# A fused attention and feed-forward kernel: lower parts, sums and stores listed elsewhere around the second product

## The chip, the cores and the metric

The kernel runs as one program on one core of a Trainium2 chip. The metric is the device time of one execution in microseconds. Before the change it is 1362.32 us, the median of 3 runs (1361.0 to 1362.66).

A core has five engines that matter here. TensorE (PE in the profile; its weight loads are PEld) multiplies matrices into PSUM. VectorE (DVE), ScalarE (ACT) and GpSimd (POOL) work on elements. SyncE (SP) only issues transfers (DMA). Each engine works through its own list of instructions in order, and waits at an instruction until what that instruction needs is done.

## The reference

```python
scores = scale * np.matmul(q, k.transpose(0, 1, 3, 2))
thresh = np.max(scores, axis=-1, keepdims=True) - tau
scores = np.where(scores >= thresh, scores, -1000000000.0)
attn = softmax(scores)                      # written out in the reference
x = (attn @ v)  ->  [4608 tokens, 512]
h = x @ w_in                                # 512 -> 2048
g = h * np.tanh(log1p(exp(h)))              # Mish
out = g @ w_out                             # 2048 -> 512
```

There are 8 batches of 8 heads, 576 positions and 64 elements a head. The first part up to x is the attention; `x @ w_in` is called the first product here, `g @ w_out` the second. Both weights arrive as 64-bit floating point numbers.

## The kernel before, in words

**Number formats.** A matrix product is made of three products of numbers split in two: each operand has an upper part in a short format and a lower part, the rest (operand minus upper part). The products upper x upper, upper x lower and lower x upper are summed in PSUM. ScalarE makes the upper parts (a cast), VectorE the lower parts (a subtraction); so a split is one ScalarE and one VectorE instruction, and the second needs the first.

**Decoding w_out.** The second weight is taken in 8 pieces, j = 0 to 7, of 128 x 1024 elements. `load_w` (line 187) brings the 64-bit words, `convert` (197) has ScalarE turn both halves into numbers, `compose` (202) has VectorE do three bit operations and GpSimd one addition, `upper_w` (212) casts on ScalarE, `lower_w` (215) subtracts on VectorE. In the profile the bit operations write `s`, `a`, `s`, the addition is `s<-s,w` on POOL, the parts are `w2h` and `w2l`.

**Units.** The attention ends near 917 us. What is left then is the first product of the last batch, 384 matmuls of 288 columns. The code deals it out in 32 units u of 12 matmuls (loop at line 804; the first four blocks of h have their last quarter held back, so the first three units finish none and unit 3 finishes four blocks, and then each unit finishes one). Between the units the table `steps` names other work: the decoding of w_out by `COMPOSE` = (0, 3, 7, 10, 14, 17, 21, 24), loads of h back from memory (`load_z`), Mish (`combine`), the split of g (`split_z`). Within a unit, the work of the table comes first, in the order in which it was put into the table, and then the 12 matmuls with what leaves them.

**How h leaves.** Each of the 32 blocks of h goes to one of 8 PSUM banks and from there into a buffer `hst`, copied by VectorE (even blocks) or ScalarE (odd blocks). A bank can be used again when it has been copied out. A buffer takes four blocks, and there are two buffers. After each fourth block `store` (545) writes the buffer to memory in two transfers.

**The second product.** It runs over 9 groups of 512 tokens (c), each over 8 pieces of the weight (j); n = 8 c + j counts the 72 steps of the loop at line 853. For c = 0 a step has 24 matmuls of 512 columns. For c > 0 the product is arranged as seven smaller products of 42 matmuls of 256 columns a step, which need four combinations of the weight's quarters: `sums_w` (219) makes them with four VectorE instructions into the free half of a z buffer, `split_w` (227) splits them (`sh` on ScalarE, `sl` on VectorE). Both run once, during c = 0. The z buffers, five of them, take turns; `load_z(n)` needs the buffer that step n - 5 had, which is free when the sums of that step are split (c = 0) or its g is split (c > 0). In each step ScalarE does Mish for step n + 3, then the upper g of step n + 2, then the upper sums of a step; after the last step of c = 0 VectorE and ScalarE copy four banks out.

**What sets the order.** The class `InOrder` (82) makes TensorE, VectorE, ScalarE and GpSimd keep the order in which the code issues. SyncE isn't wrapped, so the order of its transfers is that of the scheduler that builds the program. Because all instructions of the four engines pass through one helper, the profile shows line 92 for them; the groups are told apart by the names of their tiles.

Of the kernel before, what the change touches and what calls it, by code (L numbers as in the profile page):

```python
# [15 lines left out]
B, H, S, D = 8, 8, 576, 64  # L16
# [19 lines left out]
HB = S // 2  # L36
NBLK = 2 * B
NJ = NF // 2
# [3 lines left out]
COMPOSE = (0, 3, 7, 10, 14, 17, 21, 24)  # L42
# [35 lines left out]
def fv(ap):  # L78
    return ap.bitcast(F32)
# [78 lines left out]
def attention_moe(tc, q, k, v, tau, w_in, w_out, out):  # L158
    nc = tc.nc
    from contextlib import ExitStack  # L160

    with ExitStack() as outer:
# [56 lines left out]
        def sums_w(j):  # L219
            y = z[j]  # L220
            a11, a21, a12, a22 = (whole[j][:, i * QT:(i + 1) * QT] for i in range(4))
            nc.vector.tensor_tensor(y[:, 4], a21, a22, ALU.add)
            nc.vector.tensor_tensor(y[:, 6], a21, a11, ALU.subtract)
            nc.vector.tensor_tensor(y[:, 5], y[:, 4], a11, ALU.subtract)
            nc.vector.tensor_tensor(y[:, 7], a12, y[:, 5], ALU.subtract)

        def split_w(j):
            y = z.pop(j)[:, 4:].rearrange("p n t -> p (n t)")
            ws[j] = [
                homes["wl"].tile([P, 4 * QT], F32R, name=f"sh{j}"),  # L230
                homes["wr"].tile([P, 4 * QT], F32R, name=f"sl{j}", tag=f"sl{j}"),
            ]
            nc.scalar.copy(ws[j][0], y)
            nc.vector.tensor_tensor(ws[j][1], y, fv(ws[j][0]), ALU.subtract)

        def load_z(n):
            if n < NG:
                c, j = divmod(n, NJ)
                z[n] = scratch(CYCLE[n % 5], "z").rearrange("p (n t) -> p n t", t=QT)
                if c == 0:  # L240
                    for i in range(2):
                        nc.sync.dma_start(z[n][:, i:4:2], hd[i][:, j])
                else:
                    for at, i in ((0, 2 * c + 1), (2, 2 * c)):
                        nc.sync.dma_start(z[n][:, at:at + 2], hd[i][:, j])
# [21 lines left out]
        nc = Engines(tc)  # L267
        with ExitStack() as first:
# [6 lines left out]
            with ExitStack() as att:  # L275
# [269 lines left out]
                def store(queue, hst, at, f):  # L545

                    half, j = divmod(f, NJ)
                    off, end = 0, HB
                    while off < end:
                        i, to = divmod(at + off, QT)  # L550
                        m = min(QT - to, end - off)
                        queue.dma_start(hd[i][:, j:j + 4, half, to:to + m], hst[:, :, off:off + m])
                        off += m

                def gemm1(b, xs, bank=shared, first=1):

                    halves = (range(NF // 2), range(NF // 2, NF))  # L560
                    if b < B - 1:
                        order = [(c, f) for c in range(2) for fs in halves for f in fs]
                    else:
                        order = [(c, f) for fs in halves for c in range(2) for f in fs]
                    banks = {}
                    made = {}

                    def parts(c, f, ds):
                        if (c, f) not in banks:
                            banks[c, f] = bank("h")  # L570
                        h = banks[c, f]
                        half, at = divmod(f * P, DF // 2)
                        for d in ds:
                            xh, xl = xs[d][c]
                            wh, wl = (w[:, d, at:at + P] for w in w1[half])
                            for i, (a, m) in enumerate(((wh, xh), (wh, xl), (wl, xh))):
                                nc.tensor.matmul(
                                    h[:, :HB], a, m, start=d == 0 and i == 0, stop=d == ND - 1 and i == 2
                                )
                                yield  # L580

                    def leave(c, f):
                        if f % 4 == 0:
                            made["hst"] = hp.tile([P, 4, HB], F32, name="hst", tag="hst")
                        hst, h = made["hst"], banks.pop((c, f))
                        if b < B - 1 or f % 2:
                            nc.scalar.copy(hst[:, f % 4], h[:, :HB])
                        else:
                            nc.vector.tensor_copy(hst[:, f % 4], h[:, :HB])
                        if f % 4 == 3:  # L590
                            store(nc.sync if b < B - 1 else nc.scalar, hst, (2 * b + c) * HB, f - 3)

                    for c, f in order[:first]:
                        yield from parts(c, f, range(ND - 1))
                    for n, (c, f) in enumerate(order):
                        steps = parts(c, f, range(ND - 1, ND) if n < first else range(ND))
                        for i in range(3 if n < first else 3 * ND):
                            next(steps)
                            if i == (2 if n < first else 3 * ND - 1):
                                leave(c, f)  # L600
                            yield
# [183 lines left out]
            def at(u, *work):  # L785
                steps.setdefault(u, []).append(work)

            for j, u in enumerate(COMPOSE):
                if j >= 3:
                    at(COMPOSE[j - 3] + 2, load_w, j)  # L790
                    at(u - 2, convert, j)
                at(u, compose, j)
                at(u + 3, upper_w, j)
                at(COMPOSE[j + 1] if j + 1 < NJ else u + 4, lower_w, j)
            for n, u in enumerate((19, 20, 22, 25, 28)):
                at(u, load_z, n)
            for n, u in enumerate((22, 26, 29)):
                at(u, combine, n)
            at(24, split_z, 0)
            for _ in stream:  # L800
                pass
            stream = gemm1(B - 1, batches[B - 1], bank, 4)
# [50 lines left out]
        for n in range(NG):  # L853
            c, j = divmod(n, NJ)
            combine(n + 3)
            for i in range(n + 1 + (n > 0), n + 3):
                split_z(i)
            if n < NJ:
                sums_w(n)
                split_w(n)  # L860
            load_z(n + 5)
            if j == 0:
                banks = [bank("o") for _ in range(4 if c == 0 else len(PRODUCTS))]
            if c == 0:
                gh, gl = (x.rearrange("p n t -> p (n t)") for x in gs.pop(n))
                wh, wlo = wa[j]
                order = [(e, d) for e in range(2) for d in range(ND)]
                if j == NJ - 1:
                    order.sort(key=lambda at: at[1])
                for e, d in order:  # L870
                    cols = slice(2 * e * QT + d * P, 2 * e * QT + (d + 1) * P)
                    toks = slice(2 * e * QT, 2 * (e + 1) * QT)
                    for i, (x, y) in enumerate(((wh, gh), (wh, gl), (wlo, gh))):
                        nc.tensor.matmul(
                            banks[d], x[:, cols], y[:, toks],
                            start=j == e == i == 0, stop=j == NJ - 1 and e == 1 and i == 2,
                        )
                    if j == NJ - 1 and e == 1:
                        if d % 2 == 0:
                            pair = [x.rearrange("p n t -> p (n t)") for x in held()]  # L880
                        value = pair[d % 2]
                        if d % 2:
                            nc.vector.tensor_copy(value, banks[d])
                        else:
                            nc.scalar.copy(value, banks[d])
                        nc.sync.dma_start(out[d * P:(d + 1) * P, :2 * QT], value)
                continue
            for k, (wi, gi) in enumerate(PRODUCTS):
                o = banks[k].rearrange("p (n t) -> p n t", t=QT)
                w, at = (wa[j], (0, 2, 3)[wi]) if wi < 3 else (ws[j], wi - 3)  # L890
                for b in range(2):
                    cols = slice(at * QT + b * P, at * QT + (b + 1) * P)
                    for i, (x, y) in enumerate(((0, 0), (0, 1), (1, 0))):
                        nc.tensor.matmul(
                            o[:, b], w[x][:, cols], gs[n][y][:, gi],
                            start=j == b == i == 0, stop=j == NJ - 1 and b == 1 and i == 2,
                        )
                if j == NJ - 1:
                    leave(k, c, o)
            gs.pop(n)  # L900
# [46 lines left out]
```

## Time and profile before

| what | us |
|---|---|
| median of 3 runs | 1362.32 |
| profiled execution: its time | 1362.23 |
| profiled execution: its span | 1360.4 |
| PE busy | 1322.8 |
| DVE busy | 1112.4 |
| ACT busy | 989.4 |
| POOL busy | 874.3 |

The profile is one execution. Its span reaches from the first to the last instruction; the device time has about 1.8 us around it. Times in the views are counted from the start of the span. A row of the timeline gives start, length, engine, line, operation, tiles written and read, and in brackets how long the engine was idle before it and what ended that. The chain of waits is followed back from the last instruction: at each step it names what released it. The granted clock (PEclk) is TensorE's clock as a share of its full speed.

The stretch in question is from 917 us, when the attention has ended, to about 1043 us. From there on TensorE works without a gap until 1351.8 us.

### The profile page before, as it was taken

The page shows a single profiled execution, that of the slowest core. Times are in us where ns is not written, and L with a number is a line of the kernel's source. Part 1 is how long each engine was busy: PE and PEld are TensorE (multiplying, and loading weights), DVE is VectorE, ACT ScalarE, POOL GpSimd, SP SyncE. Part 2 cuts the span into 40 slices and gives each one's busy share as a digit, 9 for nine tenths or more (in the row PEclk, how much of TensorE's full clock was granted, in tenths as well). Part 3 has the DMA queues.
Part 4 walks back from the last instruction along what each step waited for, and adds up shares of the span by engine and source line. Part 5 has one row for each costly group of instructions (what it writes and reads, how often), then busy time and mean ns, then how long its engine had stood idle before and what let it go on. Part 6 is the DMA issues. An engine that isn't in the chain of part 4 may idle for free.

```text
span 1360.4 us, 29638 instructions
## 1 busy us (share of the span) xinstructions
PE 1322.8 (97%) x9799; PEld 1249.2 (92%) x9799; DVE 1112.4 (82%) x3018; ACT 989.4 (73%) x2052; POOL 874.3 (64%) x1191
## 2 busy tenths in 40 slices
PE   9998999999999999999999999999798999999998
PEld 7555889999999999999999999999777999999998
DVE  6999999999999999999999999965577666666664
ACT  5888788888888888888888888873555555555552
POOL 5778888788788787887878878733304334444331
PEclk9999999999999999999999999999998999999999
DMA  5333354333333333343433333215624443444440
GB/s 153 93 101 106 119 167 117 94 111 108 97 104 108 92 109 102 95 115 90 120 94 111 104 100 103 85 41 175 194 93 151 128 133 117 140 140 134 140 131 32
DMA packets 151912, 154.76 MB, mean 114 GB/s; under 512 B 35536, under 2 KB 128720, under 8 KB 151760
## 3 DMA queue, kind: packets, MB, share of 16 engines
q1 hardware_dynamic: 143312, 148.15, 36.5%
q10 hardware_dynamic: 8448, 4.72, 1.2%
q8 instruction: 78, 1.28, 0.4%
q14 instruction: 74, 0.61, 0.1%
HBM read 105.64 MB, written 47.19 MB: 112 GB/s over the span
## 4 chain that ended last, share of the span: by engine, by line
PE 85%; DVE 6%; ACT 5%; issue 2%; POOL 1%; DMA 1%; ACTq 0%; DVEq 0%; SPq 0%; POOLq 0%
PE h L92 26%; PE o L92 23%; PE s L92 13%; PE y L92 12%; PE tp L92 9%; PE t L92 1%; DVE z L92 1%; DVE st L92 1%; DVE gl L92 1%; DVE p L92 1%; POOL s L92 1%; DVE dec L92 1%; ACT gh L92 1%; ACT e L92 1%; ACT w L92 1%
## 5 line engine op out<-in xcount | busy, mean ns | idle before, releaser
L92 PE MATMUL h<-xh,w1h 128*128 128x288 f32 x1024 | 303.1, 296 | 5.2 <-DVE hst L92 4.2
L92 PE MATMUL h<-xl,w1h 128*128 128x288 f32 x1024 | 302.9, 296 | 0.0
L92 PE MATMUL h<-xh,w1l 128*128 128x288 f32 x1024 | 302.7, 296 | 0.0
L92 POOL TENSOR_SCALAR p<-p,st 128x576 f32<-128x576 f32 x288 | 244.1, 848 | 57.9 <-DVE st L92 35.1
L92 POOL TENSOR_TENSOR z<-z 128x256 f32<-128x256 f32 x128 | 130.3, 1022 | 226.4 <-DVE z L92 221.4
L92 PE MATMUL s<-k,q 128*128 128x288 f32 (+1 forms) x1280 | 254.0, 323 | 8.1 <-DVE p L92 7.9
L92 DVE SCALAR_TENSOR_TENSOR p<-s,st,e 128x576 f32<-128x576 f32 x288 | 235.1, 816 | 20.4 <-ACT e L92 10.6
L92 ACT ACTIVATE e<-s,st 128x576 f32<-128x576 f32 x288 | 214.4, 744 | 36.2 <-DVE st L92 31.4
L92 DVE TENSOR_TENSOR gl<-z,gh 128x1792 fp32r<-128x1792 f32 (+1 forms) x72 | 141.5, 1966 | 106.4 <-ACT gh L92 106.3
L92 DVE TENSOR_REDUCE st<-s 128x1 f32<-128x576 f32 x288 | 216.8, 753 | 2.7 <-PE s L92 2.6
L92 PEld LDWEIGHTS s<-k,q 128*128 128x128 f32 (+1 forms) x1280 | 181.8, 189 | 38.0 <-DVE p L92 23.5
L92 DVE TENSOR_TENSOR lo<-tp,hi 128x512 fp32r<-128x512 f32 (+1 forms) x280 | 174.9, 633 | 50.7 <-ACT hi L92 43.7
L92 ACT CAST gh<-z 128x1792 fp32r<-128x1792 f32 (+1 forms) x72 | 116.4, 1617 | 135.5 <-issue 73.3
L92 PEld LDWEIGHTS h<-xh,w1h 128*128 128x128 f32 x1024 | 193.0, 188 | 6.3 <-DVE hst L92 5.0
L92 PEld LDWEIGHTS h<-xh,w1l 128*128 128x128 f32 x1024 | 193.1, 189 | 0.0
L92 PEld LDWEIGHTS h<-xl,w1h 128*128 128x128 f32 x1024 | 193.0, 188 | 0.0
L92 PE MATMUL tp<-ident,p 128*128 128x128 f32 x1152 | 174.4, 274 | 3.5 <-DVE lo L92 2.2
L92 ACT CAST hi<-tp 128x512 fp32r<-128x512 f32 (+1 forms) x280 | 149.9, 546 | 35.3 <-PE tp L92 32.4
L92 PEld LDWEIGHTS tp<-ident,p 128*128 128x128 f32 x1152 | 138.9, 140 | 13.6 <-issue 5.4
L92 PE MATMUL o<-gh,sh 128*128 128x256 f32 x512 | 144.0, 281 | 6.1 <-ACT c L92 6.1
L92 POOL TENSOR_TENSOR x<-x,yo 64x256 f32<-64x256 f32 (+1 forms) x112 | 89.8, 802 | 89.5 <-ACT yo L92 86.3
L92 PE MATMUL o<-gh,sl 128*128 128x256 f32 x512 | 144.7, 283 | 0.0
(76 smaller groups left out, 3241.3 us busy)
## 6 DMA issues: line engine op xcount, KB each, us to landing
z<-hd SPq DMA_DIRECT2D x144, 256.0 KB, 3.1
r<-q SPq DMA_DIRECT2D x120, 160.0 KB, 2.3
r<-k SPq DMA_DIRECT2D x120, 160.0 KB, 2.2
out_t<-c SPq DMA_DIRECT2D x36, 256.0 KB, 2.4
r<-v SPq DMA_DIRECT2D x56, 160.0 KB, 2.3
dec<-w_in SPq DMA_DIRECT2D x32, 256.0 KB, 3.3
w<-w_out SPq DMA_DIRECT2D x16, 512.0 KB, 4.4
hd<-hst SPq DMA_DIRECT2D x12, 512.0 KB, 3.3
```

The source lines that it names most:

```text
L92: made = method(*args, **kwargs)
```

## The change

Four things are listed elsewhere; no instruction is added or removed.

1. `lower_w(j)` is listed one unit later: not in the unit of `compose(j + 1)`, where it stood ahead of it, but in the unit after. The last one, j = 7, stays.
2. `sums_w` for j = 0, 1, 2 is listed in units 26, 29 and 31 of the first product; for j = 3 to 7 it is listed in steps n = 1 to 5 of the second product, two steps ahead of step n = j. `split_w(j)` is listed in step n = j - 1 (j = 0 and j = 1 both in step 0). Within a step the sums come after the split of g, and the split of the sums after these.
3. `load_z` runs six steps ahead instead of five; step 0 issues two.
4. The last batch's `store` is issued from SyncE's list, not ScalarE's.

```diff
-                            store(nc.sync if b < B - 1 else nc.scalar, hst, (2 * b + c) * HB, f - 3)
+                            store(nc.sync, hst, (2 * b + c) * HB, f - 3)
...
                 at(u, compose, j)
                 at(u + 3, upper_w, j)
-                at(COMPOSE[j + 1] if j + 1 < NJ else u + 4, lower_w, j)
+                at(COMPOSE[j + 1] + 1 if j + 1 < NJ else u + 4, lower_w, j)
...
             at(24, split_z, 0)
+            for j, u in enumerate((26, 29, 31)):
+                at(u, sums_w, j)
...
             combine(n + 3)
             for i in range(n + 1 + (n > 0), n + 3):
                 split_z(i)
-            if n < NJ:
-                sums_w(n)
-                split_w(n)
-            load_z(n + 5)
+            if 0 < n < NJ - 2:
+                sums_w(n + 2)
+            for i in range(n + (n > 0), min(n + 2, NJ)):
+                split_w(i)
+            for i in range(n + 5 + (n > 0), n + 7):
+                load_z(i)
```

## The prediction

> **What bounds the kernel now.** I read the page first, then TensorE's waits after the attention, then the granted clock where they lie, then the chain of waits through them.
>
> ```profile
> span 1360.4 us, 29638 instructions
> PE 1322.8 (97%) x9799; PEld 1249.2 (92%) x9799; DVE 1112.4 (82%) x3018; ACT 989.4 (73%) x2052; POOL 874.3 (64%) x1191
> ```
>
> TensorE is busy for 97% of the span, so only its waits, and the slow clock after them, can be won. All edits act after 917 us. The waits of PE from 925 us to the end (us in total, times, longest):
>
> ```profile
> PE o L92 <- ACT c L92: 6.1, 1, 6.1
> PE o L92 <- issue: 5.2, 1, 5.2
> PE h L92 <- DVE hst L92: 4.2, 3, 1.8
> PE o L92 <- ACT gh L92: 1.9, 1, 1.9
> PE o L92 <- DVE gl L92: 0.8, 1, 0.8
> ```
>
> That is 18.2 us in seven waits: three in the first product of the last batch (banks of h not yet copied out), three where the second product starts, one of 6.1 where it goes from its first to its second column group, which I call the seam. After the long ones the clock is halved (stage; its length, busy times, then PEclk):
>
> ```profile
> 979.10:981.90 2.80, 2.80 (x7) 2.25 (x8) 0.27 (x1) 0.98 (x2) 1.79 (x1) 0.50 0.02 6
> 988.00:992.14 4.14, 3.37 (x8) 2.48 (x9) 3.78 (x6) 1.20 (x2) 0.00 (x0) 0.59 0.01 2
> 1038.38:1043.34 4.96, 4.96 (x23) 4.94 (x24) 4.48 (x5) 3.07 (x4) 2.28 (x2) 0.50 0.77 249
> ```
>
> Length times missing clock: 1.4 + 1.7 + 2.5 = 5.6 us. So 23.8 us are there to be won, and no more.
>
> The Trainium skill (TensorE: Matmul & The Clock Gate, "What's actually happening") lets the clock fall after a full idle window of about 3.4 us. By that rule the 1.9 us wait would have cost no clock and the ceiling would be 1.7 lower; the second row above, 0.59 behind a wait of 1.9, disagrees, and I keep the row.
>
> Why the first six exist shows in one step of decoding the second weight, as the chain has it (start, length):
>
> ```profile
> 951.22 1.11 issue
> 952.32 0.70 DVE s L92
> 953.04 0.71 DVE a L92
> 953.77 1.24 DVE s L92
> 955.14 2.45 POOL s L92
> 957.61 1.06 ACT w2h L92
> 958.73 1.11 issue
> ```
>
> The pieces called issue are VectorE's lower parts, which the chain doesn't name. It is a ring: lower part of j-1, three bit operations of step j, GpSimd's add, ScalarE's upper part, lower part of j: 7.51 us a step. PE gives a step 3.5 units of 12 matmuls:
>
> ```profile
> 932.29 18.87 PE h L92 x140
> ```
>
> 18.87 / 140 = 0.135 us, 1.62 a unit, 5.7 a step. Eight banks hide the ring's lag until h's copies, listed behind the ring on VectorE, come too late.
>
> **The change, part by part.** (1) *Lower parts one unit later*: no instruction more. Lower j now stands behind the bits of j+1, so VectorE no longer waits out add and upper part between them; the ring is cut. What remains is what VectorE and GpSimd can do together, and that is little:
>
> ```profile
> 977.42 1.22 DVE L92 TENSOR_TENSOR gl<-z,gh 128x1024 fp32r<-128x1024 f32 x1
> 977.63 3.26 POOL L92 TENSOR_TENSOR s<-s,w 128x1024 uint32<-128x1024 uint32 x1 [5.07 <-DVE s L92]
> ```
>
> ```profile
> 1017.63 1.22 DVE L92 TENSOR_TENSOR gl<-z,gh 128x1024 fp32r<-128x1024 f32 x1
> 1017.70 1.75 POOL L92 TENSOR_TENSOR z<-z 128x256 f32<-128x256 f32 x1 [36.81 <-DVE z L92]
> 1018.77 0.96 DVE L92 TENSOR_TENSOR z<-s 128x256 f32<-128x256 f32 x1
> ```
>
> An add that takes 2.45 alone takes 3.26 when a split runs: it ends 2.25 after the split's end at 978.64. The second group shows both sides held: POOL ends (1019.45) 0.6 after the split's end, and VectorE's next, of some 0.35 alone (the chain's row of three below), takes 0.96 behind it. Copies out of PSUM are not held:
>
> ```profile
> 931.78 0.46 DVE L92 COPY hst<-h 128x288 f32<-128x288 f32 x1
> 931.82 2.42 POOL L92 TENSOR_TENSOR s<-s,w 128x1024 uint32<-128x1024 uint32 x1 [5.01 <-DVE s L92]
> ```
>
> This speaks against the change, which puts bits and lower parts beside the adds. I count VectorE's SBUF work and the adds one after the other. The bit operations beside an add are not in these rows; bounds are no hold and full hold, and I take full hold, nearest to the two rows of the same engines. The Trainium skill (SBUF — State Buffer, "Who interferes with whom") says the same: the shared pair is locked for a whole instruction and the other engine blocks; by it the sum is the one that follows, without it that of the first rival.
>
> The first operation of step 0 starts at 921.54:
>
> ```profile
> 921.54 0.69 DVE L92 TENSOR_SCALAR s<-w 128x1024 f32<-128x1024 f32 x1 [7.99 <-POOL xl L92]
> ```
>
> From there to the end of the second split of g, with which PE may start its second step of the second product: 8 x 2.65 (bits) = 21.2; 8 x 2.3 (adds, held) = 18.4; 8 x 1.11 (lower) = 8.9; two splits, 2.4; three sums, which part (2) moves here, 4 operations each of which three take 1.01 below, so 3 x 1.45 = 4.4. Together 55.3. The 16 copies of h take 0.4 each, 6.4; those listed straight after the bits lie beside the add. I let 2 us of them count (bounds 0 and 6.4). 921.5 + 57.3 = 978.8, taken as 979.
>
> Does PE wait before? Copy 0 comes after two steps of bits and one add: 921.5 + 7.6 + 0.4 = 929.5; PE wants the bank at 932.29 - 1.77 (the wait's length) = 930.5. Just in time. Each later step costs VectorE and GpSimd 6.1 to 6.5 against 5.7, so the lag grows but is under the lead of eight banks: the three waits of 4.2 go, and PE ends the first product at 930.5 + 288 x 0.135 = 969.4. Then it needs copies 24 to 27. Copy 24, after the bits of step 7 and the first split, comes at 921.5 + 21.2 + 16.1 + 6.7 + 1.2 + 2 = 968.7, in time; copy 26, behind another add, lower part and sum, some 5 later, where PE, three matmuls a bank, wants it at 970.8. So **a new wait of about 3 us** stands there, and a second before the second split. Steps of PE cost, by the rows
>
> ```profile
> 1028.65 0.39 PE L92 MATMUL o<-gh,w2h 128*128 128x512 f32 x1
> 1028.88 0.39 PE L92 MATMUL o<-gl,w2h 128*128 128x512 f32 x1
> 1029.11 0.39 PE L92 MATMUL o<-gh,w2l 128*128 128x512 f32 x1
> 1029.35 0.28 PE L92 MATMUL o<-gh,w2h 128*128 128x256 f32 x1
> ```
>
> 24 x 0.233 = 5.6. Seven more from 979 end at 1018.2, where the second column group begins; before, it began at 1029.35 (last row). **Gain 11.1.** Undisturbed, from 969.4 with eight steps, it would be 1014.2, gain 15.1.
>
> (2) *Sums two steps ahead of their split*. The loop of the first column group is a ring too:
>
> ```profile
> 1004.20 1.06 ACT z L92
> 1005.26 0.94 ACT gh L92
> 1006.23 1.23 DVE gl L92
> 1007.45 1.01 DVE z L92 x3
> 1009.33 0.57 issue
> ```
>
> Mish, upper g, lower g, sums, upper sum, next mish at 1009.90: 5.7 a step, over PE's 5.6. So the chain arrives at the last step without a lead, and the copies of the first group's banks stand behind it: that is the 6.1. With the sums already there, ScalarE has 1.06 + 0.94 + 1.0 = 3.0 a step and VectorE 1.23 + 1.45 + 1.23 = 3.9 of 5.6 (holds by GpSimd come on top from the fifth step, under 2.5). The last split of sums moves to the step before, so nothing but a mish and one g stands before the copies, which start as the banks end. **The seam goes: 6.1 + 2.5 of clock = 8.6.** If the cover is gone (a loop over 5.6 a step) it comes back. The loads of z one step earlier wait for the split of sums one step earlier, so they gain.
>
> (3) *Last stores on SyncE*. Sixteen transfers leave ScalarE's list, where each waited for VectorE's copies with everything behind it:
>
> ```profile
> 948.06 2.16 ACT L92 ACTIVATE w<-w 128x1024 f32<-128x1024 f32 x2 [4.98 <-DVE hst L92]
> ```
>
> 4.98 us is the price of one such wait, and it delays a convert. Alone this is worth little now; with (1) it keeps ScalarE from handing VectorE's lag back. On SyncE's queue they stand among the loads, which are not in the order written:
>
> ```profile
> 950.15 2.03 SPq L242 DMA_DIRECT2D z<-hd x4
> 957.61 1.07 SPq L192 DMA_DIRECT2D w<-w_out x2
> ```
>
> (z is written after this w.) So I can't read the new order. Taking 0.5 us an issue (2.03 / 4), 16 cost 8 us of a queue that is mostly waiting: nothing, unless a store stands behind a load that waits. Two buffers of h give each store about 8 us (five units) before the copy that reuses its buffer, against a landing of 3.18:
>
> ```profile
> 971.65 3.18 DMA hd<-hst
> ```
>
> **Sum.** 11.1 + 8.6 = 19.7. The profiled execution took 1362.23 (span 1360.4), next to the median of 1362.32. 1362.3 - 19.7 = 1342.6; 1342.9 with 0.3 for a clock halved by the new wait, which mostly falls where PE waits for the split anyway. Its own range is 1341 to 1345.5.
>
> **Rivals.** *No hold between VectorE and GpSimd*: both product starts undisturbed, gain 15.1 + 8.6 = 23.7, 1338.6. The rows above speak against it. *A later start of the second product*: all copies count (4.4 more) and the clock halves once more (1.7): 1347 to 1349; for it speaks that every item stands on one engine's list. *The seam stays*, the change not doing there what it says: a loop with GpSimd's holds over 5.6 would do it; 1342.9 + 8.6 = 1351.5; against it speaks the 3.9. *It evens out*: new waits eat all 19.7, 1362; nothing seen for it. *Slower*: on SyncE a store stands behind a load of w that waits for an add. Then copies of h wait for a buffer, bits wait behind the copies, the add behind the bits, and the load for that add: a new ring of issues 1.0, landing 3.18, copy 0.4, bits 2.65, add 2.45 = 9.7 a step. Eight are 77.6, ending at 999; with the last lower parts, sums and splits (10) the second step starts at 1009, 30 later than forecast: 1372.9. It decides once a store is held for over the 5 us of slack in every step. For it: the order is not the written one; against it: the transfers come in the trace as their conditions came true.
>
> **How the numbers follow.** Forecast 58%, no hold 12%, later start 17%, seam 5%, evened out 4%, slower 4%. The likeliest gives **1342.9**. From 1337.5 to 1349 holds forecast, no hold and later start, 87% less their fringes. About 0.2% is what a measurement of this kernel can tell from no change. Faster: 92%; same: 3%; slower: 5% (the slower rival and a share of the evened-out).
>
> **What would show it.** Right: no wait of PE on hst between 925 and 969; the first product's end near 969; a short wait on hst or gl between 969 and 979; the second column group from about 1018 with no wait of 6 and full clock; adds of 3 us and more beside bits or lower parts. Wrong: adds at 2.45 beside bits (no hold); the first 512-column matmul after 972; a wait on ScalarE's copies at the seam; z or w loads in SyncE's list with stores held behind them.

## The result, and the profile after

| kernel | median us | runs | ratio to before, 95% interval |
|---|---|---|---|
| before | 1361.88 | 4 (1361.0 to 1362.66) | |
| changed | 1342.44 | 4 (1341.68 to 1342.51) | 0.9856 (0.9839 to 0.9873) |

The kernel is 19.4 us faster; the profiled execution took 1341.68 us with a span of 1339.9. The forecast was 1342.9 (1341 to 1345.5).

The page of the changed kernel, first part, and then TensorE's waits from 925 us to the end (us in total, times, longest):

```profile
span 1339.9 us, 29650 instructions
...
PE 1317.0 (98%) x9799; PEld 1244.9 (93%) x9799; DVE 1123.4 (84%) x3018; ACT 989.0 (74%) x2052; POOL 872.7 (65%) x1191
```

```profile
PE o L92 <- DVE hst L92: 3.2, 1, 3.2
```

Each of the engines listed has as many instructions as before; the 12 more in the first line are none of theirs. Of seven waits with 18.2 us one is left, with 3.2. TensorE's busy time falls too, by 5.8 us from 1322.8 to 1317.0, though it does the same 9799 matmuls: 4.0 of that is slow clock, 5.6 before less the 1.6 below. The chain of waits says where the one wait stands and what it follows (start, length):

```profile
966.40 1.22 DVE gl L92
967.62 0.37 DVE hst L92
967.98 3.00 DVE w2l L92
970.98 1.02 DVE z L92 x3
```

This is VectorE's list from the first split of g on: the split, copy 24, the lower part of step 6, the sums of j = 0, and then copy 26, for which TensorE waits with its third bank. The lower part takes 3.00 us in place of 1.2; why is seen below. The clock around this wait, by stage (length, busy times, PEclk):

```profile
967.00:972.80 5.80, 2.71 (x16) 2.11 (x15) 5.77 (x9) 3.12 (x7) 2.90 (x1) 0.98 0.61 184
972.80:976.20 3.40, 3.33 (x8) 2.65 (x9) 3.37 (x9) 3.40 (x5) 0.00 (x0) 0.52 0.61 189
976.20:979.70 3.50, 3.50 (x16) 2.66 (x16) 3.47 (x6) 3.22 (x4) 0.00 (x0) 1.00 0.56 171
```

3.40 us at 0.52 are 1.6 us of work lost. So 3.2 + 1.6, 4.8 us, are all that TensorE still loses between 925 us and the end. The seam, as the timeline has it:

```profile
1017.36 0.39 PE L92 MATMUL o<-gh,w2l 128*128 128x512 f32 x1
1017.60 0.28 PE L92 MATMUL o<-gh,w2h 128*128 128x256 f32 x1
```

The second column group starts at 1017.60 (before: 1029.35) and runs through; no wait on ScalarE's copies is left in the list above. Of the 11.8 us between the two, 0.5 lies ahead of the stretch: the first product of the last batch begins at 917.09, not at 917.61. Counted from there the second column group begins after 100.5 us, where before it began after 111.7: 11.2 won, against a forecast of 11.1. From the second column group to the end of the span it is 322.3, before 331.05: 8.75 won, against 8.6.

The hold that the forecast rests on shows at the first place where bits and addition now meet. VectorE and GpSimd at the first two steps of the decoding:

```profile
923.61 0.69 DVE L92 TENSOR_SCALAR s<-w 128x1024 f32<-128x1024 f32 x1
923.86 2.73 POOL L92 TENSOR_TENSOR s<-s,w 128x1024 uint32<-128x1024 uint32 x1 [2.88 <-DVE s L92]
924.33 2.80 DVE L92 TENSOR_SCALAR a<-s 128x1024 uint32<-128x1024 uint32 x1
```

The bit operation that begins at 924.33 takes 2.80 us; before the change it took 0.69. It ends 0.5 after the addition does (926.59). The addition in its turn takes 2.73, 0.3 more than alone, since it had to wait for the operation begun at 923.61. So bit operations are held too, which no row of before had shown, and the hold lasts until the addition ends.

### The profile page after: what moved, and what is told of

Its sections match the earlier page's. It is cut to its first block, busy times and chain, and to the rows that moved or that the text cites. A ratio compares the mean times of both kernels' runs of the same rounds, so it can differ in the third digit from the quotient of the medians.

```text
span 1339.9 us, 29650 instructions
## 1 busy us (share of the span) xinstructions
PE 1317.0 (98%) x9799; PEld 1244.9 (93%) x9799; DVE 1123.4 (84%) x3018; ACT 989.0 (74%) x2052; POOL 872.7 (65%) x1191
## 4 chain that ended last, share of the span: by engine, by line
PE 90%; DVE 5%; ACT 3%; issue 1%; DMA 1%; POOL 0%; DVEq 0%; ACTq 0%; POOLq 0%; SPq 0%
PE o L92 27%; PE h L92 27%; PE s L92 14%; PE y L92 12%; PE tp L92 9%; DVE st L92 1%; PE t L92 1%; DVE p L92 1%; DVE dec L92 1%; DVE w2l L92 1%; ACT e L92 1%; PE warm L92 1%; ACT w L92 0%; ACT dec L92 0%; DMA hd<-hst 0%
## 5 line engine op out<-in xcount | busy, mean ns | idle before, releaser
L92 POOL TENSOR_TENSOR z<-z 128x256 f32<-128x256 f32 x128 | 124.4, 976 | 223.0 <-DVE z L92 214.2
L92 DVE SCALAR_TENSOR_TENSOR p<-s,st,e 128x576 f32<-128x576 f32 x288 | 235.1, 816 | 20.4 <-ACT e L92 10.4
L92 PE MATMUL o<-gl,sh 128*128 128x256 f32 x512 | 143.8, 281 | 0.0
```

Of the source, the lines that this page charges most:

```text
L92: made = method(*args, **kwargs)
```

## The experiments

Part 1, 2 and 3 are those of the prediction: part 1 is item 1 of the change, part 2 items 2 and 3, part 3 item 4. My theory, H below: in this stretch VectorE's work on SBUF and GpSimd's additions exclude each other, and their sum sets when the second product gets going. The rivals: N, no exclusion, and the rest of the loss is VectorE's own list; Q, it is SyncE's order, stores behind loads. All ratios below are to the kernel before, timed beside each run (medians 1362.1 for the first four, 1361.13 for the last four).

**The addition twice.** The cost in dispute, doubled: the extra addition writes words that nobody reads again.

```diff
+            nc.gpsimd.tensor_tensor(top, b, low, ALU.add)
             nc.gpsimd.tensor_tensor(b, b, low, ALU.add)
```

> The changed kernel with GpSimd's addition in each decoding step made twice, the first time into words that nobody reads any more (2.45 us more of GpSimd in each of 8 steps; nothing of the result is left out). Theory H (VectorE's SBUF work and GpSimd's additions exclude each other, so the stretch from 921 to the second split of g is their sum): 8 x 2.3 = 18 us more in that sum, of which ScalarE and VectorE copies hide a little; the second step of the second product starts 15 to 18 us later and the time is 1342.4 + 16 = 1358 (1355 to 1361). Theory N (no exclusion; the 5 us still lost are VectorE's own list): GpSimd has 4.9 us in a step of 5.7, the additions stay beside VectorE's work, and the time is 1342.4 to 1344. Theory Q (the loss is SyncE's order: stores behind loads that wait for additions): the loads start 2.4 us later each, a few us, 1345 to 1350.

Measured: 1358.62 us (8 runs, 1357.25 to 1359.05), ratio 0.9974 (0.9964 to 0.9985): 16 us of the 19.4 are gone, as H says. TensorE's waits from 925 us on:

```profile
PE o L92 <- issue: 6.6, 1, 6.6
PE h L92 <- ACT hst L92: 3.8, 4, 1.4
PE h L92 <- DVE hst L92: 3.0, 5, 1.1
PE o L92 <- DVE hst L92: 1.9, 1, 1.9
```

The waits are back in the first product and at its end, and VectorE's rows tell why:

```profile
924.16 2.81 DVE L92 TENSOR_SCALAR a<-s 128x1024 uint32<-128x1024 uint32 x1
927.00 3.33 DVE L92 SCALAR_TENSOR_TENSOR s<-s,a 128x1024 uint32<-128x1024 uint32 x1
```

Two bit operations of 0.69 and 1.23 take 2.81 and 3.33, one behind each addition. GpSimd would have had room (4.9 us in a step of 5.7), so N, which gave 1344 at most, falls. Q's 1350 is passed as well: the only wait of VectorE for a store in that stretch is one of 2.5 us, in front of copy 20, so the queue accounts for 2.5 of the 16 at most.

**The addition away from GpSimd.** VectorE makes it as a bitwise or. For that the low word is scaled so that it rounds into the three free bits; the last bit of a decoded weight can differ.

```diff
-            nc.scalar.activation(low, low, AF.Copy, scale=2.0**-29)
+            nc.scalar.activation(low, low, AF.Copy, scale=0.93 * 2.0**-29)
...
-            nc.gpsimd.tensor_tensor(b, b, low, ALU.add)
+            nc.vector.tensor_tensor(b, b, low, ALU.bitwise_or)
```

> The changed kernel with the addition taken from GpSimd and made on VectorE as a bitwise or (the low word is scaled by 0.93 more, so that it rounds into the three bits that are free; the last bit of a weight can differ). Theory H: VectorE pays 1.14 us a step and 2.3 us of exclusion go, 8 x 1.16 = 9 us less in the sum, more than the 5 us that TensorE still loses; the wait before the third bank and the slow clock behind it go: 1337.5 (1337 to 1339). Theory N: VectorE's list gets 8 x 1.14 = 9 us longer and nothing goes: 1342 to 1351. Theory Q: the loads follow the shorter chain, 1340 to 1342.

Measured: 1336.98 us (4 runs, 1336.32 to 1339.1), ratio 0.9819 (0.9804 to 0.9833), which is 5.5 us under the changed kernel, at the lower end of H's range and below what N and Q gave. From 925 us on TensorE waits for nothing. VectorE has got more to do, and it is quicker through:

```profile
927.29 1.23 DVE L92 TENSOR_TENSOR s<-s,w 128x1024 uint32<-128x1024 uint32 x1
928.55 0.82 DVE L92 COPY hst<-h 128x288 f32<-128x288 f32 x2
929.29 1.22 DVE L92 TENSOR_TENSOR w2l<-s,w2h 128x1024 fp32r<-128x1024 f32 x1
```

The or costs 1.23 in place of a hold that was put at 2.3, and the lower part behind it is 1.22 again, where the changed kernel's first one took 2.83 (begun at 929.17). The bit operation that took 2.80 takes 0.69 here. The run also takes the way over GpSimd out of each step, so by its time alone it can't tell the hold from a shorter chain; these rows can. This version beats both kernels.

**The stores on ScalarE again** (part 3 undone).

```diff
-                            store(nc.sync, hst, (2 * b + c) * HB, f - 3)
+                            store(nc.sync if b < B - 1 else nc.scalar, hst, (2 * b + c) * HB, f - 3)
```

> The changed kernel with the last batch's stores issued from ScalarE again (part 3 undone). Theory H: each store waits on ScalarE for VectorE's copies, which are late because of the exclusion, and delays the upper parts, Mish and upper g behind it; 3 to 5 us later: 1346 (1344.5 to 1348). Theory N: VectorE has a lead, the stores wait for nothing: 1342 to 1343. Theory Q: the stores can't be held behind loads any more, so it is faster: 1339 to 1341.5.

Measured: 1345.17 us (4 runs, 1343.82 to 1345.71), ratio 0.9874 (0.986 to 0.9889): 2.7 us over the changed kernel. ScalarE's rows show the cost:

```profile
969.85 0.39 ACT L92 COPY hst<-h 128x288 f32<-128x288 f32 x1
973.37 0.93 ACTq L92 DMA_DIRECT2D hd<-hst  x2
974.40 1.07 ACT L92 ACTIVATE z<-z 128x1024 f32<-128x1024 f32 x1 [4.15 <-issue]
```

The store of blocks 24 to 27 stands from 970.2 to 973.4 for VectorE's copy 26, with Mish and the last copies behind it. So ScalarE hands VectorE's lag on, and TensorE waits 6.4 us in four places. Q had it faster; it is slower.

**The lower parts alone** (part 1 on the kernel before).

```diff
-                at(COMPOSE[j + 1] if j + 1 < NJ else u + 4, lower_w, j)
+                at(COMPOSE[j + 1] + 1 if j + 1 < NJ else u + 4, lower_w, j)
```

> The kernel before with the lower parts one unit later and nothing else (part 1 alone). Theory H: the ring is cut, the second product starts about 11 us earlier, less what the stores on ScalarE give back; the seam of 6 us and its slow clock stay: 1361.9 - 10 = 1352 (1350 to 1354). Theory N: the second product starts undisturbed, 14 to 15 us earlier: 1347 to 1348. Theory Q: as N or better.

Measured: 1353.04 us (4 runs, 1350.79 to 1353.91), ratio 0.9931 (0.9914 to 0.9947), a gain of 9.1. The waits:

```profile
PE o L92 <- ACT c L92: 6.5, 1, 6.5
PE o L92 <- ACT hst L92: 2.3, 1, 2.3
PE o L92 <- ACT gh L92: 1.9, 1, 1.9
PE o L92 <- DVE gl L92: 0.8, 1, 0.8
```

Nothing is left in the first product (h); the ring is cut. The seam stays.

**The sums alone** (part 2 on the kernel before; the diff is that of the change in `steps` and in the loop over n).

```diff
+            for j, u in enumerate((26, 29, 31)):
+                at(u, sums_w, j)
...
-            if n < NJ:
-                sums_w(n)
-                split_w(n)
-            load_z(n + 5)
+            if 0 < n < NJ - 2:
+                sums_w(n + 2)
+            for i in range(n + (n > 0), min(n + 2, NJ)):
+                split_w(i)
+            for i in range(n + 5 + (n > 0), n + 7):
+                load_z(i)
```

> The kernel before with part 2 alone (sums two steps ahead of their split, loads of z six steps ahead). Theory H and the forecast alike: the seam goes with its slow clock (8.6 us), the start of the second product stays as before or 0.5 us later for the sums listed there: 1362 - 8.5 = 1353.5 (1352.5 to 1355). Rival (the seam was held by something else, a load of z or the banks): 1360 or more.

Measured: 1352.31 us (4 runs, 1351.45 to 1352.99), ratio 0.9932 (0.9917 to 0.9947), a gain of 8.8. The waits:

```profile
PE o L92 <- issue: 5.2, 1, 5.2
PE h L92 <- DVE hst L92: 2.6, 2, 1.8
PE o L92 <- DVE gl L92: 0.8, 1, 0.8
PE o L92 <- DVE hst L92: 0.7, 1, 0.7
```

The seam's 6.1 is gone and the start of the second product is as late as before: the mirror of the run above. The waits up to there have become shorter (9.3 us, before 12.1), but the clock was slow for longer: behind the wait of 1.8 at 930 us it was 0.50 from 933 to 935 us, where before, behind a wait as long, it was 1.00.

**The stores alone** (part 3 on the kernel before; its diff is that of the stores above, turned round).

> The kernel before with part 3 alone (the last batch's stores on SyncE). Theory H: ScalarE no longer waits with convert and upper parts behind VectorE's copies; the ring stays, so little: 1 to 3 us of the first product and of the start of the second, 1359 (1358 to 1361). Rival (stores on SyncE are held behind loads and hold the copies): 1362 or more.

Measured: 1357.76 us (7 runs, 1356.61 to 1358.57), ratio 0.9973 (0.9962 to 0.9984), a gain of 3.4. That is more than I had expected (1 to 3 us), and the time lies outside the 1358 to 1361 that I had given. The waits:

```profile
PE o L92 <- ACT c L92: 6.8, 1, 6.8
PE o L92 <- issue: 5.2, 1, 5.2
PE h L92 <- DVE hst L92: 2.1, 2, 1.8
```

In the ring as it was, a store's wait on ScalarE already cost TensorE something: of the 4.2, 1.9 and 0.8 of the kernel before, 2.1 are left. The 5.2 and the seam stay.

**Part 1 undone, and part 2 undone.** The diffs are those of the two parts above, turned round, on the changed kernel.

> The changed kernel with part 1 undone (lower parts ahead of the next step's bits again). Theory H: the ring of 7.5 us is back, and with it the waits in the first product and at the start of the second; the seam stays closed: 1342.4 + 8 = 1350.5 (1349 to 1352.5). Rival (the stores alone held the ring): 1344 or less.

> The changed kernel with part 2 undone (sums in the step of their split, loads of z five steps ahead). Theory H: the seam comes back, 8.6 us, less 1.5 to 2 us because the three sums no longer stand before the copies of h at the end of the first product: 1342.4 + 7 = 1349.4 (1348 to 1351). Rival (the earlier start of the second product closes the seam by itself): 1341 to 1343.

Measured: without part 1 1350.3 us (4 runs, 1349.34 to 1351.3), ratio 0.992 (0.9903 to 0.9938); without part 2 1347.34 us (4 runs, 1346.65 to 1349.15), ratio 0.9898 (0.9882 to 0.9914). The first lies in its range, the second below its range of 1348 to 1351. The waits without part 1:

```profile
PE o L92 <- issue: 5.2, 1, 5.2
PE h L92 <- DVE hst L92: 3.4, 3, 1.8
PE o L92 <- DVE hst L92: 0.7, 1, 0.7
```

The ring's waits in the first product and at the start of the second are back, and the seam stays closed. The waits without part 2:

```profile
PE o L92 <- ACT c L92: 7.4, 1, 7.4
PE o L92 <- DVE hst L92: 1.7, 1, 1.7
```

The seam is back and longer than before (7.4 to 6.1), since TensorE now comes to it earlier and the loop with the sums is no quicker; and the wait for copy 26 is 1.7, not 3.2, since the sums of j = 0 no longer stand in front of it. By the ratios (the kernel before ran 0.75 us quicker beside these runs than beside the changed kernel) taking part 2 away costs (0.9898 - 0.9856) x 1362 = 5.7 us and taking part 1 away 8.7. I had expected 7 and 8. Each of these ratios is known to about 2 us, so the 1 us missing from the 7 is less than they can tell. The profiled executions, cut at the start of the second column group and counted from the first matmul of the last batch's first product, show the parts more sharply (us):

| kernel | to the second column group | from there to the end |
|---|---|---|
| before | 111.7 | 331.05 |
| before with part 1 | 102.8 | 331.3 |
| before with part 2 | 111.5 | 322.5 |
| before with part 3 | 107.9 | 331.0 |
| changed, part 1 undone | 109.2 | 322.3 |
| changed, part 2 undone | 97.7 | 332.0 |
| changed, part 3 undone | 104.4 | 322.3 |
| changed | 100.5 | 322.3 |

Parts 1 and 3 act in the first column; in the second only part 2 makes a difference of more than 1 us. But part 2 has a price in the first: undone, it gives back 2.8 us there and costs 9.7 at the seam, 6.9 together. Its three sums stand in VectorE's list ahead of copy 26, and without them the wait for that copy is 1.7 and the clock stays at 1.00 behind it; with them it is 3.2, and the clock falls to half.

Each part alone gains 9.1, 8.8 and 3.4 by the medians, together 21.3; all three gain 19.4. By the table parts 1 and 3 don't save the same waits: alone they win 9.0 and 3.9 in the first column, both without part 2 win 14.0, and all three 11.2. So what is lost when the three meet is the price of part 2, which doesn't show in the kernel before (111.7 and 111.5), where the ring holds VectorE up anyway. A version that lists the three sums behind copy 26 was not run.

What wasn't settled: what the hold of a store on SyncE costs. A third buffer for h would tell; no such version was run.

## Why the prediction was right

**The ceiling.** Waits of 18.2 and a slow clock of 5.6 gave 23.8 to be won. 19.4 are won, 4.8 are left (3.2 and 1.6): 24.2. The version with the or, in which TensorE waits for nothing, gains 24.7, by its ratio and by its profile counted as in the table. So "no more" was about 1 us too strict: the listed waits and stages don't hold all that TensorE lost.

**Part 1: the ring and what is left of it.** The step that decided was to count VectorE and GpSimd one after the other, though only splits and sums, not bits, had been seen beside an addition. The first rival, no hold, would have given 1338.6. The changed kernel's row of 2.80 shows bits held, and the doubled addition moves the time by 16 us, where 8 x 2.3 = 18 were put in. By the Trainium skill (SBUF — State Buffer, "Who interferes with whom") the shared pair is locked for a whole instruction; the rows agree, for additions behind bits and for bits behind additions.

The stations of the sum, forecast and measured: copy 0 at 929.5, measured 928.9 (a row of VectorE's, 928.43 and 0.45 long); no wait in the first product, and there is none; its end at 969.4, measured 968.2, when the first matmul of the second product starts:

```profile
968.17 0.39 PE L92 MATMUL o<-gh,w2h 128*128 128x512 f32 x1
```

The rate comes from a row of the chain:

```profile
917.25 23.95 PE h L92 x180
```

180 matmuls in 23.95 are 0.133 each, not the 0.135 I took from a row whose last matmul runs past the rest; over 288 matmuls that is 0.5 us, and the whole execution stands some 0.5 us earlier. Then the wait of about 3 us for copy 26: 3.2. The second wait, for the second split of g, is too short to be listed; there the clock, slow for 3.4 us behind the first wait, took the same time. The second column group at 1018.2: 1017.60. So the path was right, station by station. Inside the sum two terms were off and made up for each other. By their rows, VectorE's operations took 14.0 us longer beside the eight additions than alone, where 18.4 stood for the additions, and its 16 copies of h took 5.9, where 2 were counted. That is no luck, since a copy that lies beside an addition takes up a part of the hold: 19.9 together against 20.4.

**Part 2: the seam.** Put at 8.6, alone it gains 8.8, and from the second column group to the end 331.05 became 322.5. Right, by the term it was put at. The three sums that it moves were counted too, as 4.4 us of VectorE's list in part 1; undoing the part showed 2.8 us of that at the second column group.

**Part 3: the stores.** "Alone this is worth little now" was too low: alone 3.4 us. With part 1 "it keeps ScalarE from handing VectorE's lag back" was right and is worth 2.7 us.

**SyncE's order.** The slower rival needed a store held behind a load that waits for an addition, in every step and for over 5 us. It does occur, once, by SyncE's rows and one of VectorE's:

```profile
943.91 6.93 SPq L192 DMA_DIRECT2D w<-w_out  x3
950.95 1.54 SPq L552 DMA_DIRECT2D hd<-hst  x2
```

```profile
956.90 0.46 DVE L92 COPY hst<-h 128x288 f32<-128x288 f32 x1 [0.87 <-DMA hd<-hst]
```

Among the three transfers of w in the first row is one that waited for an addition's end; the store behind it came at 950.95, and copy 20 waited 0.87 us for a buffer. The mechanism was real: the store came 2.7 us after the copy it needed (copy 14 ended at 948.29), and it took 5.9 from issue to landing, where issue and landing had been put at 4.2. The slack of five units swallowed all but 0.87 of it, in one step of eight. That 0.87 cost VectorE next to nothing, since copy 20 lies beside the addition that runs from 954.66 to 957.95: the bit operation behind the copy ended at 958.50, 0.5 after the addition, as the one in the first step did.

**The slow clock behind the new wait.** I let 0.3 us count for it, since the split would come no earlier. It was 1.6 us of work, but it fell where TensorE would have waited for the second split: the split ended at about 978.74 (begun at 977.52, 1.22 long), and the matmul that needs it started at 978.80. The second step itself began at 978.54, not at 979. The term was too small, and the error cost nothing, because the one hid the other. The prediction had named that ("mostly falls where PE waits for the split anyway"); that the two came out equally long is luck.

## What to carry to other kernels

Where two engines exclude each other, a ring that is cut between them comes back as the sum of their work: cost them as one engine before judging what a reordering can win. It then pays to ask which of the two does a piece of work in less time, not which of the two is idle; here VectorE, at 84% busy, made GpSimd's addition, as a bitwise or, in half the time (1.23 to 2.45) and the kernel 5.5 us faster. What is listed early to feed a later stage has its price in the stage where it is listed, here 2.8 us. And a transfer that waits for another engine's copies belongs on a list with nothing urgent behind it.

## What the runs showed of the hardware that I had not expected

- Integer bit operations of VectorE on 128 x 1024 words, both the tensor-scalar (0.69 us) and the two-tensor form (1.23), wait out an addition on GpSimd: 2.80 and 3.33 us. Copies out of PSUM beside an addition keep their 0.45.
- A wait of 3.2 us, with TensorE running before and after it, halved the clock for 3.4 us (0.52 in that stage). In the kernel before, a wait of 1.9 with one of 0.8 close behind did the same, and waits of 1.6 to 1.8 alone in the first product did not. The length alone doesn't decide it: with the sums alone a wait of 1.79 in the same place was followed by half clock (0.50 from 933 to 935 us), with the stores alone too (0.60 from 931 to 933), and with part 1 undone the same 1.79 was not. A wait of 2.3 at the start of the second product, with part 3 undone, was not either. What else decides it no run here shows.
